# A three-stage token kernel on one core: the second stage in seven products of quarters, with three weights decoded early and staged in DRAM

## The chip, the cores and the metric

The kernel runs on one core of one Trainium2 chip. The metric is device time in microseconds (us) of one execution. The core has separate instruction streams for TensorE (PE, with its weight loads as PEld), VectorE (DVE), ScalarE (ACT), GpSimd (POOL) and SyncE (SP, which issues nearly all DMAs here). The fast memory on the core is SBUF, matmul results go to PSUM, and the chip's DRAM holds inputs, outputs and whatever is staged between.

## The reference

Attention gives 2304 tokens of 512 numbers each; two layers follow.

```python
x = attention(q, k, v)            # pooled (factor 4) attention plus a banded local one, 4 batches of 576 tokens
h = (x @ w_a) * (x @ w_b)         # 512 -> 1536
x2 = h @ w_out                    # 1536 -> 512, the second stage
g = x2 @ w_in                     # 512 -> 2048, the third
g = g * clip(g + 3, 0, 6) / 6
out = g @ w_out2                  # 2048 -> 512, the fourth
```

Weights arrive as 64-bit floats and are decoded on the chip into 32-bit ones. A product of float32 matrices is done in three passes: each operand is split in two parts of fewer bits (ACT copies the first part, DVE subtracts to get the second), and first x second, second x first and first x first are added up in PSUM.

## The kernel before

**The order of the work** comes from a planner. Every step (`PE`, `ACT`, `DVE` or `DMA`) is added with an estimated cost, a wanted time, the steps it follows and the buffers it takes and gives back. The planner then walks through time and issues, on each engine, the ready step that is wanted earliest; the engine executes them in just that order. Times in the plan only decide the order, and a wait on the chip is a semaphore.

**Stage 1** works on blocks of at most 384 tokens. Attention for two units of 116 tokens after the other makes the block's tile `x` (in two parts: `total` L603, `x_first` L611 on ACT, `x_second` L616 on DVE). Three such tiles exist. For a block, `job` runs through 12 column groups of w_a and w_b: two products of 12 matmuls each into `pab` (L663), a copy on ACT (L669), a multiplication on DVE (L672) and a store of `h` to DRAM (L675). Attention of the later blocks is woven between these products on PE: scores `sc` and `dsc`, transposes `pt` and `dpt`, and products with v, `po` L590 and `dpo`.

**Weights.** `decode` loads a tile of 128 x 1024 doubles (as two 32-bit words each) into one of three `raw` slots and makes floats of it: absolute value on ACT (L262), two exponent passes on DVE (L276, L277), a rounding pass on ACT (L270, some on DVE, L268), the upper word's pass L281 and the joining pass L287 on DVE. For w_a, w_b and w_out the two parts then go straight to SBUF (L291, L294). `pieces` decodes the second layer's first weight w_in, makes four sums of quarters on DVE (L330) and splits seven pieces (L339, L343). `staged` decodes the second layer's second weight, eight tiles, makes four differences of quarters (L1142) and writes seven pieces to DRAM in three DMAs (`w_d`), wanted from shortly before the time T1 in stage 1; stage 4 reads them back.

**Stage 2**, `second(n, f, want)`, goes through spans of 512 tokens (four, and one of 256) and, in each, through 12 tiles of `h`: a load (L704), the split on ACT (L708) and DVE (L712), and 4 x 3 matmuls into four PSUM banks (L720). After the twelfth tile ACT copies the result out (L752) and it goes to DRAM as `x2_d`.

**Stages 3 and 4** already work in seven products of quarters: two blocks of 384 tokens and two halves of the inner dimension form a 2 x 2 matrix of blocks, and seven products in place of eight, of sums and differences, give the result. `inner` and its `group` do it with 1008 matmuls of 384 columns (L848), `outer` with 1512 of 256 (L972, L987). The operands are split at L775 and L778 after a subtraction of 128x768 (L784); the results are put together at L857, L865, L873 and L876.

Of the kernel before, what the change touches and what calls it, by code (L numbers as in the profile page):

```python
# [9 lines left out]
F32 = mybir.dt.float32  # L10
# [144 lines left out]
def fused_kernel(ctx: ExitStack, tc: tile.TileContext, qk, vt, vd, wab, wo, w2i, w2o, mask, out):  # L155
# [33 lines left out]
    def fill():  # L189
        if not unread:  # L190
# [8 lines left out]
            "eT": 2, "xf": 2, "x": 3, "a": 3, "b": 4, "s2": 2, "wo": F1 // 2, "w2": 2, "hg0": 2,  # L199
            "hg1": 2, "xo": 3, "q": 8, "ws": 1, "x0": 4, "L": 24, "c": 14}  # L200
# [3 lines left out]
    plan.loose |= {"b", "turn", "pv", "m", "s2", "e", "de", "eT", "deT", "xf", "dqk", "a", "q", "xo", "c"}  # L204
# [37 lines left out]
    wab_t, wo_t, w2_t = {}, {}, {}  # L242
# [69 lines left out]
    takers = {}  # L312

    def pieces(src, want, where, raw=None, step=CUT):


        i, words = decode(src, want, None, None, slack=1.0, raw=raw, step=step)
        Q = W // CUT

        def quarters():  # L320
            lo, hi = words()
            return (hi.bitcast(F32).rearrange("p (a c) -> p a c", a=CUT),
                    lo.bitcast(F32).rearrange("p (a c) -> p a c", a=CUT))

        def sums():
            v, e = quarters()
            for k, (x, y, op) in enumerate(
                    ((v[:, 2], v[:, 3], ALU.add), (e[:, 0], v[:, 0], ALU.subtract),
                     (v[:, 0], v[:, 2], ALU.subtract), (v[:, 1], e[:, 1], ALU.subtract))):
                nc.vector.tensor_tensor(e[:, k], x, y, op=op)  # L330

        i = DVE(4 * dve(Q), want, sums, [i], slack=1.0)

        ends = []
        for at, of, q, n in ((0, 0, 0, 2), (2, 0, 3, 1), (3, 1, 0, 4)):
            for a, b, key, tag, before, place in where(at, at + n):
                def first(a=a, b=b, of=of, q=q + a - at, place=place):
                    x = quarters()[of][:, q:q + b - a]
                    nc.scalar.activation(place(0), x, AF.Copy)  # L339

                def second(a=a, b=b, of=of, q=q + a - at, place=place):
                    x = quarters()[of][:, q:q + b - a]
                    nc.vector.tensor_tensor(place(1), x, place(0), op=ALU.subtract)  # L343

                n_ = (b - a) * Q
                j = ACT(act(n_), want, first, [i, *before, takers.get(key)], take=[tag] if tag else [], slack=1.0)
                takers.setdefault(key, j)
                ends.append(DVE(dve(n_), want, second, [j]))
        return plan.add("-", 0, want, lambda: None, ends, give=[raw or "raw"])

# [334 lines left out]

    cuts = list(range(0, NT, NC)) + [NT]
    spans = list(zip(cuts, cuts[1:]))
    hs, accs, x2_d = {}, {}, {}

    def hg_slot(n, f, name):  # L690
        if n == 0 and f in EDGE:
            return slot(xp, [P, 2, NC], F32R, "x", name)
        return slot(pools["p3" if f % 4 > 1 else "p2"], [P, 2, NC], F32R, f"hg{f % 4 // 2}", name)

# [3 lines left out]
    def second(n, f, want):  # L698
        lo, hi = spans[n]
        nb = hi - lo  # L700

        def load():
            h = hs[n, f] = hg_slot(n, f, "h")[:, :, :nb]
            nc.sync.dma_start(h[:, 1].bitcast(F32), h_d[f][:, lo:hi])  # L704

        def h_first():
            h = hs[n, f]
            nc.scalar.activation(h[:, 0], h[:, 1].bitcast(F32), AF.Copy)  # L708

        def h_second():  # L710
            h = hs[n, f]
            nc.vector.tensor_tensor(h[:, 1], h[:, 1].bitcast(F32), h[:, 0], op=ALU.subtract)  # L712
# [10 lines left out]
        edge = n == 0 and f in EDGE  # L723
        hg = "x" if edge else f"hg{f % 4 // 2}"
        stored = [x for m in range(NBLK) if begin[m] < hi and begin[m] + sizes[m] > lo for x in S_["h", m, f]]
        i = DMA(nb // 2, want - 40, load, stored + ([] if edge else [S_["p3" if f % 4 > 1 else "p2"]]), take=[hg])
        i = ACT(act(nb), want - 14, h_first, [i])
        i = DVE(dve(nb), want - 14, h_second, [i])
        busy = 12 * (0.0134 + nb / 2400)
        end = n == len(spans) - 1  # L730
        take, give = ["q"] * KC if f == 0 else [], [hg]
        if end and f >= F1 - 3:

            i = S_["issued", f] = PE(0.01, want - 3, products, [i, S_["wo", f // 2], S_["ps"], S_.get(("issued", f - 1))],
                                     take=take, slack=-PE_L)
            i = PE(busy, want, lambda: None, [i], give=give)
        else:
            i = PE(busy, want, products, [i, S_["wo", f // 2], S_["ps"], S_["second", n, 0] if f else None], take=take, give=give)
        S_["second", n, f] = i
        if f < F1 - 1:  # L740
            return
        if end:
            S_["p4"] = plan.add("-", 0, 0, open_p4, [S_["issued", f]] +
                                [issued[x] for m in range(2 * PAIRS) for x in S_.get(("x2d", m), [])] +
                                [issued[x] for k in range(F2 // 2) for x in S_["w_d", k]])
        for e in range(KC):
            T = {}

            def out_of(e=e, T=T):
                T["t"] = (slot(pools["p4"], [P, NB], F32, "c", "x2f") if end else  # L750
                          slot(pools["p3"], [P, NC], F32, "xo", "x2f"))[:, :nb]
                nc.scalar.activation(T["t"], accs[n][e], AF.Copy)  # L752

            def store(e=e, T=T):
                for m in range(lo // NB, (hi - 1) // NB + 1):
                    if m not in x2_d:
                        x2_d[m] = dram.tile([KC, P, NB], F32, name=f"x2_d{m}")
                    a, b = max(lo, m * NB), min(hi, m * NB + NB)
                    nc.sync.dma_start(x2_d[m][e][:, a - m * NB:b - m * NB], T["t"][:, a - lo:b - lo])

            tag = "c" if end else "xo"
            j = ACT(act(nb), want, out_of, [i, S_["p4"] if end else None], take=[tag], give=["q"])
            j = DMA(nb // 2, want, store, [j], give=[tag])
            for m in range(lo // NB, (hi - 1) // NB + 1):
                S_.setdefault(("x2d", m), []).append(j)
# [20 lines left out]
    def inner(p, want, opened):  # L786
# [49 lines left out]
    def group(p, i, want, X, ready):  # L836
# [3 lines left out]
        def product(k, w, give=(), onto=None, after=()):  # L840
# [10 lines left out]
            return PE(6 * (0.0134 + NB / 2400), w, run, ready[k] + [S_["w2i", i], S_["ps"], *after],  # L851
# [266 lines left out]
    w_d = [dram.tile([P, 7, CUT, W // CUT], F32, name=f"w_d{h}") for h in range(F2 // 2 // CUT)]  # L1118

    def staged(k, want):  # L1120
        i, words = decode(w2o[k], want, None, None, slack=1.0, step=1)
        T = {}

# [205 lines left out]
```

## Time and profile before

| | before |
|---|---|
| runs shown (us) | 941.47, 940.19, 939.75; median 940.19 |
| the profiled execution: its time (us) | 938.81 |
| its span, first to last instruction (us) | 936.7 |
| PE busy | 925.9 us, 99% of the span |
| PEld busy | 867.6 us, 93% |
| DVE busy | 659.2 us, 70% |
| ACT busy | 511.2 us, 55% |
| DMA, mean over the span | 161 GB/s |

Start and end of the profiled execution lie 2.1 us outside its span. Busy time is time in which an engine had an instruction in it, so it is a share of the whole, over stages with different limits; matmuls are pipelined, so that one matmul's own duration (335 ns, say) is longer than the distance from one to the next. The stages follow each other in time: stage 1 to 425.9 us, stage 2 to 576.9 us, stage 3 to 752.2 us, then stage 4.

### The profile page before, as it was taken

To read this page: it belongs to the slowest core of one execution; us is meant where nothing else is said; L and a number is where in the kernel's file an instruction comes from. 1 tells how busy PE (TensorE), PEld (TensorE's weight loads), DVE (VectorE), ACT (ScalarE), POOL (GpSimd) and SP (SyncE) were. 2 spreads that over 40 slices of the span, in tenths; PEclk is the share of its full clock that TensorE was granted. 3 is DMA by queue.
4 is the path that set the end of the run, shared out by engine and by line. 5 is a ranking of instruction groups with operands and counts; after the bars stand their busy time and mean duration, and the time that the engine had idled before them with its cause. 6 is when DMAs were issued, how large, how long until landed. Compare 5 with 4: busy or idle time off the path is not lost.

```text
span 936.7 us, 18571 instructions
## 1 busy us (share of the span) xinstructions
PE 925.9 (99%) x7040; PEld 867.6 (93%) x7040; DVE 659.2 (70%) x1231; ACT 511.2 (55%) x1242; POOL 3.2 (0%) x40
## 2 busy tenths in 40 slices
PE   9999999999999999999999999999999999999998
PEld 6678899999999999997888889999999999999998
DVE  5999967767967677789222224777556799897983
ACT  3768744557557654455322324666566775454551
POOL 0000000000000000000000000000000000000000
PEclk9999999999999999999999999999999999999999
DMA  9734845555554454554434544525257782706401
GB/s 299 238 121 158 284 169 170 169 170 169 192 182 162 130 190 140 180 159 129 135 100 137 140 122 133 186 94 194 103 182 244 265 265 72 261 7 208 130 19 51
DMA packets 102440, 151.20 MB, mean 161 GB/s; under 512 B 8784, under 2 KB 70992, under 8 KB 102352
## 3 DMA queue, kind: packets, MB, share of 16 engines
q1 hardware_dynamic: 101632, 148.80, 49.2%
q8 instruction: 55, 0.90, 0.4%
q10 hardware_dynamic: 720, 1.23, 0.4%
q14 instruction: 33, 0.27, 0.1%
HBM read 100.19 MB, written 49.81 MB: 160 GB/s over the span
## 4 chain that ended last, share of the span: by engine, by line
PE 92%; DVE 5%; DMA 1%; ACT 1%; issue 0%; SPq 0%; POOL 0%; ACTq 0%; POOLq 0%; DVEq 0%
PE pab L663 31%; PE ph L848 19%; PE oacc L987 18%; PE acc L720 16%; PE po L590 2%; PE dsc L433 2%; PE dpo L483 1%; PE oacc L972 1%; PE sc L534 1%; PE dpt L465 1%; PE unread L192 1%; PE pt L575 1%; DMA raw<-w2o 1%; DVE dqk L423 1%; DVE raw L287 0%; DVE m L281 0%
## 5 line engine op out<-in xcount | busy, mean ns | idle before, releaser
L663 PE MATMUL pab<-x,wh 128*128 128x384 f32 (+2 forms) x1776 | 320.2, 337 | 0.1
L663 PEld LDWEIGHTS pab<-x,wh 128*128 128x128 f32 x1776 | 302.0, 188 | 3.4 <-issue 1.3
L848 PE MATMUL ph<-in,w 128*128 128x384 f32 x1008 | 175.3, 335 | 0.0
L848 PEld LDWEIGHTS ph<-in,w 128*128 128x128 f32 x1008 | 175.1, 188 | 0.0
L987 PE MATMUL oacc<-w2o,in 128*128 128x256 f32 x1440 | 172.6, 283 | 0.0
L987 PEld LDWEIGHTS oacc<-w2o,in 128*128 128x128 f32 x1440 | 172.6, 192 | 0.0
L720 PE MATMUL acc<-h,wo 128*128 128x512 f32 (+1 forms) x720 | 150.9, 371 | 1.4 <-DVE a L672 1.1
L720 PEld LDWEIGHTS acc<-h,wo 128*128 128x128 f32 x720 | 125.4, 188 | 27.0 <-DVE a L672 1.4
L712 DVE TENSOR_TENSOR h<-h 128x512 fp32r<-128x512 f32 (+1 forms) x60 | 38.1, 638 | 98.2 <-ACT h L708 98.2
L708 ACT ACTIVATE h<-h 128x512 fp32r<-128x512 f32 (+1 forms) x60 | 35.3, 589 | 94.1 <-DMA h<-h_d 57.5
L672 DVE TENSOR_TENSOR a<-a,pab 128x384 f32<-128x384 f32 (+2 forms) x74 | 40.0, 540 | 59.4 <-PE pab L663 31.7
L669 ACT ACTIVATE a<-pab 128x384 f32<-128x384 f32 (+2 forms) x74 | 35.6, 480 | 81.4 <-PE pab L663 70.9
L775 ACT ACTIVATE in<-gr 128x384 fp32r<-128x384 f32 x96 | 47.3, 520 | 41.7 <-PE oacc L987 27.3
L865 DVE TENSOR_TENSOR part<-ph,part 128x384 f32<-128x384 f32 x72 | 39.8, 555 | 32.5 <-PE ph L848 21.2
L873 ACT ACTIVATE r<-part,three 128x384 f32<-128x384 f32 x72 | 43.9, 615 | 27.4 <-DVE part L865 26.5
L778 DVE TENSOR_TENSOR in<-gr,in 128x384 fp32r<-128x384 f32 x96 | 49.6, 551 | 8.0 <-ACT in L775 7.5
L775 ACT ACTIVATE in<-e 128x384 fp32r<-128x384 f32 x72 | 37.1, 524 | 29.1 <-PE oacc L987 22.7
L857 ACT ACTIVATE part<-ph 128x384 f32<-128x384 f32 x72 | 35.2, 490 | 27.0 <-PE ph L848 25.2
L262 ACT ACTIVATE m<-raw 128x1024 f32<-128x1024 f32 x34 | 38.8, 1140 | 7.0 <-DMA raw<-w2o 2.6
L281 DVE SCALAR_TENSOR_TENSOR m<-raw,m 128x1024 uint32<-128x1024 uint32 x34 | 41.4, 1218 | 0.3
L287 DVE CUSTOM_DVE_ANT_0 raw<-raw,m 128x2048 uint16<-128x2048 uint16 x34 | 41.3, 1216 | 0.3
L876 DVE SCALAR_TENSOR_TENSOR r<-r,part 128x384 f32<-128x384 f32 x72 | 38.8, 549 | 0.9 <-ACT r L873 0.9
(97 smaller groups left out, 966.8 us busy)
## 6 DMA issues: line engine op xcount, KB each, us to landing
g_d<-r SPq DMA_DIRECT2D x96, 192.0 KB
gr<-g_d SPq DMA_DIRECT2D x48, 384.0 KB
h_d<-a SPq DMA_DIRECT2D x70, 192.0 KB
raw<-wab SPq DMA_DIRECT2D x12, 1024.0 KB
h<-h_d SPq DMA_DIRECT2D x48, 256.0 KB
raw<-w2o SPq DMA_DIRECT2D x32, 256.0 KB
w2o<-w_d SPq DMA_DIRECT2D x14, 512.0 KB
qk<-qk SPq DMA_DIRECT2D x12, 576.0 KB
```

The lines of the kernel that those rows point to most:

```text
L262: nc.scalar.activation(T["m"], words()[1].bitcast(F32), AF.Abs)
L281: nc.vector.scalar_tensor_tensor(out=mu, in0=words()[1], scalar=0xC0000000, in1=mu, op0=ALU.bitwise_and, op1=ALU.bitwise_or)
L287: nc.vector.tensor_tensor(hi, T["m"].bitcast(U32), lo, op=ALU.add)
L663: nc.tensor.matmul(T[k], wab_t[f][:, x, c], xs[n][:, g, y, ja:jb], start=(g == 0 and i == 0), stop=(g == KC - 1 and i == 2))
L672: nc.vector.tensor_tensor(T["a"], T["a"], T[1], op=ALU.mult)
L720: nc.tensor.matmul(accs[n][e], wo_t[f // 2][:, x, c], hs[n, f][:, y], start=(f == 0 and i == 0), stop=(f == F1 - 1 and i == 2))
L775: nc.scalar.activation(x[0][:, 0], src(), AF.Copy)
L778: nc.vector.tensor_tensor(x[0][:, 1], src(), x[0][:, 0], op=ALU.subtract)
L848: nc.tensor.matmul(acc[k], t[:, x, g * P:(g + 1) * P], X[k, g][0][:, y], start=(g == 0 and n == 0 and not onto), stop=(g == 1 and n == 2), ...
L865: nc.vector.tensor_tensor(s[name], acc[k], s[other], op=ALU.add)
L873: nc.scalar.activation(T["r"], src(), AF.Relu, bias=three)
L987: nc.tensor.matmul(acc[n][e], X[n, k][0][:, x, e * P:(e + 1) * P], t[:, y], start=(k == 0 and i == 0), stop=(k == K - 1 and i == 2))
```

## The change

**Stage 2** becomes `middle(p)`, three times, each for a pair of 384-token blocks. h for a pair (two blocks of tokens, t = 0 and 1) and w_out are both cut into quarters (the inner dimension in two halves of six tiles), and seven products are formed in the order 1, 5, 6, 3, 7, 2, 4. Each product is three steps (kk) of 12 matmuls of 384 columns (two tiles of h, two of the four output tiles, three passes), 36 in all; so 63 steps and 756 matmuls stand where 720 stood, 576 of them of 512 columns and 144 of 256. `load` brings four DMAs of 192 KB per kk and block of tokens, the first block into `h0`, the second into a `raw` slot of `decode`. For each product `sub` subtracts on DVE in place where a difference is wanted, and `parts` splits into one of six `X` slots, 128x768 each time. `keep` copies a PSUM result to SBUF on ACT, `add` adds the next product's to it on DVE, and products marked `onto` go on in the same PSUM bank.

**Weights.** w_out and w_in are now `staged` as well, before the second layer's second weight: 22 tiles in all, wanted from T1 - LEAD - SOON on, one every PACE. A tile is decoded in its `raw` slot, four sums or differences are written on DVE (L1170), three quarters copied on ACT (L1173), and the seven pieces leave as one DMA of 896 KB; `raw` is given back when that has landed. `loaded` brings them back as tiles `wt` of 512 KB, 11 for w_out and 14 for w_in, and splits them on ACT (L1230) and DVE (L1234). `pieces` and the direct way of w_out go.

The core of the diff:

```diff
-            "eT": 2, "xf": 2, "x": 3, "a": 3, "b": 4, "s2": 2, "wo": F1 // 2, "w2": 2, "hg0": 2,
-            "hg1": 2, "xo": 3, "q": 8, "ws": 1, "x0": 4, "L": 24, "c": 14}
+            "eT": 2, "xf": 2, "x": 3, "a": 3, "b": 4, "s2": 2, "h0": 3, "X": 6, "y": 8, "w2": 2, "q": 8, "x0": 4, "L": 24,
+            "c": 14}
...
-        def products():
-            if f == 0:
-                accs[n] = [bank("acc")[:, :nb] for _ in range(KC)]
-            for e in range(KC):
-                c = slice(f % 2 * DM + e * P, f % 2 * DM + (e + 1) * P)
-                for i, (x, y) in enumerate(PASSES):
-                    nc.tensor.matmul(accs[n][e], wo_t[f // 2][:, x, c], hs[n, f][:, y],
-                                     start=(f == 0 and i == 0), stop=(f == F1 - 1 and i == 2))
...
+            e1 = parts(1, kk, b11, [l0])
+            t1 = sub(5, b11, b12, b11, [e1, l1])
+            e5 = parts(5, kk, b11, [t1])
+            t2 = sub(6, b11, b22, b11, [e5])
+            e6 = parts(6, kk, b11, [t2])
+            e3 = parts(3, kk, b22, [l1])
+            t3 = sub(7, b12, b22, b12, [e3, t1])
+            e7 = parts(7, kk, b12, [t3])
+            plan.add("-", 0, want, lambda: None, [e7, t2], give=["raw"])
+            e2 = parts(2, kk, b21, [l0])
+            t4 = sub(4, b11, b21, b11, [e2, e6])
+            e4 = parts(4, kk, b11, [t4])
...
+                    for j in range(2):
+                        t = wo_t[(c0 + j) // CUT][:, (c0 + j) % CUT]
+                        for e in range(2):
+                            for i, (x, y) in enumerate(PASSES):
+                                nc.tensor.matmul(acc[n][e], t[:, x, e * P:(e + 1) * P], X[n, kk][:, j, y],
+                                                 start=(kk == 0 and j == 0 and i == 0 and not onto),
+                                                 stop=(kk == KK - 1 and j == 1 and i == 2), skip_group_check=n != 2)
...
-    for k in range(F2 // 2):
-        S_["w_d", k] = staged(k, T1 - 16 + 2.4 * k)
+        j = ACT(act(3 * Q), want, copy, [i])
+        k = DVE(4 * dve(Q), want, sums, [i], slack=0.3)
+        plan.add("-", 0, want, lambda: None, [j, k], give=["dm"])
+        return [DMA(896, want, lambda: nc.sync.dma_start(dest, r7()), [j, k], give=["raw"])]
...
+        S_[name, k] = staged(src[k], T1 - LEAD - SOON + PACE * i, dest(), name == "w_d")
...
+        S_["wo", j] = loaded((T2 - 34 + 2.5 * j, T2 - 30 + 2.5 * j), "wh", parts_, made, lambda t, j=j: wo_t.setdefault(j, t))
```

How this moves instructions shows best in stage 1, where block 3 of the tokens (the fourth block) begins. In before, the stream of DVE there has the last split of that block's `x` (L616, twice) among work for the block being multiplied (L672) and for attention:

```order
L672 TENSOR_TENSOR a<-a,pab 128x384
L423 TENSOR_REDUCE dqk<-qk 128x288
L1142 TENSOR_TENSOR ws<-raw,ws 128x256
L281 SCALAR_TENSOR_TENSOR m<-raw,m 128x1024
L603 TENSOR_TENSOR xf<-po,od 128x464
L565 TENSOR_SCALAR z<-z 128x8
L566 RECIPROCAL z<-z 128x8
L438 TENSOR_REDUCE dmx<-dsc 72x4
L441 TENSOR_SCALAR dmx<-dmx 72x4
L616 TENSOR_TENSOR x<-xf,x 128x4x36
L616 TENSOR_TENSOR x<-xf,x 128x4x80
L375 TENSOR_TENSOR e<-e,z 128x512
```

In the changed kernel the same split (now L578) has four decode passes (L277, L278, L282, L289) and a row maximum (L511, L512) between it and the multiplication ahead (now L634), which is the last one of block 2:

```order
L634 TENSOR_TENSOR a<-a,pab 128x384
L277 TENSOR_SCALAR m<-m 128x1024
L278 TENSOR_SCALAR m<-m 128x1024
L511 TENSOR_REDUCE mx<-e 128x8
L512 TENSOR_SCALAR mx<-mx 128x8
L282 SCALAR_TENSOR_TENSOR m<-raw,m 128x1024
L565 TENSOR_TENSOR xf<-po,od 128x464
L289 ISA m<-raw,m 128x2048
L578 TENSOR_TENSOR x<-xf,x 128x4x36
L578 TENSOR_TENSOR x<-xf,x 128x4x80
L400 TENSOR_REDUCE dmx<-dsc 72x4
L403 TENSOR_SCALAR dmx<-dmx 72x4
```

The split has moved back, behind the end of block 2's products. On PE, in before, block 3's last attention product `po_3110` is followed by five more products of block 2 (`x_1550`) and some attention work; the first product of block 3, `pab_3325<-x_2820`, comes four rows after this piece:

```order
L590 MATMUL po_3110<-eT_3099,vz1_104 64x58 x16
L433 MATMUL dsc_3134<-dqk_3106 72x144 x4
L663 MATMUL pab_3145<-x_1550,wh_1807 128x384 x12
L663 MATMUL pab_3175<-x_1550,wh_2014 128x384 x12
L575 MATMUL pt_3193<-ident_81,e_3041 128x128 x4
L663 MATMUL pab_3202<-x_1550,wh_2014 128x384 x12
L590 MATMUL po_3220<-eT_3217,vz0_103 64x58 x16
L465 MATMUL dpt_3241<-ident_81,de_3167 72x72 x4
L433 MATMUL dsc_3247<-dqk_3190 72x144 x4
L663 MATMUL pab_3255<-x_1550,wh_2098 128x384 x12
L465 MATMUL dpt_3283<-ident_81,de_3167 72x72 x4
L663 MATMUL pab_3288<-x_1550,wh_2098 128x384 x12
```

In the changed kernel that attention product (`po_3236`) comes after the last product of block 2 (`x_1560`), and the first of block 3 (`x_2880`) right behind it:

```order
L625 MATMUL pab_3145<-x_1560,wh_2160 128x384 x12
L625 MATMUL pab_3170<-x_1560,wh_2355 128x384 x12
L625 MATMUL pab_3196<-x_1560,wh_2355 128x384 x12
L537 MATMUL pt_3221<-ident_81,e_3068 128x128 x4
L395 MATMUL dsc_3229<-dqk_3218 72x144 x4
L552 MATMUL po_3236<-eT_3226,vz1_104 64x58 x16
L625 MATMUL pab_3281<-x_2880,wh_434 128x384 x12
L625 MATMUL pab_3311<-x_2880,wh_434 128x384 x12
L625 MATMUL pab_3334<-x_2880,wh_640 128x384 x12
```

Between block 3's last attention product and its first use there is nothing left on PE. The third place is DVE early in stage 2 of the changed kernel, with the differences (L700), the second parts (L683) and second parts of weights (L1234):

```order
L700 TENSOR_TENSOR hr<-hr 128x768 x2
L683 TENSOR_TENSOR hx<-hr,hx 128x2x384 x3
L700 TENSOR_TENSOR hr<-hr 128x768
L1234 TENSOR_TENSOR wt<-wt 128x4x256 x2
L683 TENSOR_TENSOR hx<-hr,hx 128x2x384 x3
L700 TENSOR_TENSOR hr<-hr 128x768
L683 TENSOR_TENSOR hx<-hr,hx 128x2x384
L700 TENSOR_TENSOR hr<-hr 128x768
L683 TENSOR_TENSOR hx<-hr,hx 128x2x384
L700 TENSOR_TENSOR hr<-hr 128x768
L683 TENSOR_TENSOR hx<-hr,hx 128x2x384
L1234 TENSOR_TENSOR wt<-wt 128x4x256
```

Where before DVE had one second part (L712) for twelve matmuls, it now has one of 128x768 and, for more than every second step, a difference of the same size as well, in turns.

## Rows read from the trace of the kernel before

**Rows 1.** Cores: span, mean granted TensorE clock.
```profile
core 0: 936.7 us, clock 1.000
```
**Rows 2.** Chain of work that ended last: start us, us, what.
```profile
425.88 136.12 PE acc L720 x600
...
577.07 175.18 PE ph L848 x1008
```
**Rows 3.** Windows: us, then PE, PEld, DVE, ACT, POOL busy; PEclk, DMA share, GB/s.
```profile
80.00:245.00 165.00, 164.15 (x1459) 153.94 (x1458) 127.99 (x222) 100.55 (x293) 1.27 (x16) 1.00 0.58 191
425.90:576.90 151.00, 150.70 (x720) 125.40 (x721) 52.22 (x85) 49.41 (x84) 0.00 (x0) 1.00 0.44 129
576.90:752.20 175.30, 175.30 (x1011) 175.30 (x1010) 123.28 (x231) 115.85 (x224) 0.00 (x0) 1.00 0.52 176
```
**Rows 4.** Lines by form, PE and PEld: busy us, mean ns, idle before.
```profile
L848 PE MATMUL ph<-in,w 128*128 128x384 f32 x1008 | 175.3, 335 | 0.0
L848 PEld LDWEIGHTS ph<-in,w 128*128 128x128 f32 x1008 | 175.1, 188 | 0.0
...
L720 PEld LDWEIGHTS acc<-h,wo 128*128 128x128 f32 x720 | 125.4, 188 | 27.0 <-DVE a L672 1.4 <-ACT h L708 0.4 <-DVE h L712 0.3
```
**Rows 5.** Timeline of DVE around 245 us: start us, us, operation.
```profile
245.05 0.70 DVE L616 TENSOR_TENSOR x<-xf,x 128x144 fp32r<-128x144 f32 x2
```
**Rows 6.** Timeline of PE from 236 to 260 us: start us, us, operation.
```profile
247.38 0.60 PE L575 MATMUL pt<-ident,e 128*128 128x128 f32 x4
...
249.98 1.14 PE L590 MATMUL po<-eT,vz 64*64 64x58 f32 x32
...
257.45 0.71 PE L433 MATMUL dsc<-dqk 64*72 64x144 f32 x8
258.09 2.18 PE L663 MATMUL pab<-x,wh 128*128 128x384 f32 x11
```
**Rows 7.** Lines by form, DVE operations of stage 1.
```profile
L281 DVE SCALAR_TENSOR_TENSOR m<-raw,m 128x1024 uint32<-128x1024 uint32 x34 | 41.4, 1218 | 0.3
L287 DVE CUSTOM_DVE_ANT_0 raw<-raw,m 128x2048 uint16<-128x2048 uint16 x34 | 41.3, 1216 | 0.3
...
L672 DVE TENSOR_TENSOR a<-a,pab 128x384 f32<-128x384 f32 x70 | 38.6, 551 | 58.5 <-PE pab L663 31.0 <-ACT m L262 12.2 <-ACT wo L291 4.9
...
L277 DVE TENSOR_SCALAR m<-m 128x1024 uint32<-128x1024 uint32 x34 | 23.6, 694 | 1.2
L276 DVE TENSOR_SCALAR m<-m 128x1024 f32<-128x1024 f32 x34 | 23.2, 682 | 1.1 <-ACT m L262 1.1
...
L330 DVE TENSOR_TENSOR raw<-raw 128x256 f32<-128x256 f32 x32 | 12.1, 421 | 0.3
...
L549 DVE TENSOR_REDUCE mx<-e 128x8 f32<-128x512 f32 x10 | 6.7, 673 | 0.0
...
L603 DVE TENSOR_TENSOR xf<-po,od 128x464 f32<-128x464 f32 x9 | 5.6, 625 | 2.0 <-PE po L590 1.5 <-PE sc L534 0.5
...
L550 DVE TENSOR_SCALAR mx<-mx 128x8 f32<-128x8 f32 x20 | 3.4, 171 | 0.7
```
**Rows 8.** Waits: who waited for whom, us in total, times, longest.
```profile
DVE h L712 <- ACT h L708: 98.2, 52, 3.1
...
PE acc L720 <- DVE a L672: 1.1, 1, 1.1
```
**Rows 9.** Lines by form: operations of the sizes that the new stage uses.
```profile
L865 DVE TENSOR_TENSOR part<-ph,part 128x384 f32<-128x384 f32 x72 | 39.8, 555 | 32.5 <-PE ph L848 21.2 <-ACT in L775 5.2 <-ACT part L857 5.2
...
L1250 DVE TENSOR_TENSOR w2o<-w2o 128x1024 fp32r<-128x1024 f32 x14 | 17.0, 1216 | 1.0 <-ACT w2o L1246 1.0
...
L784 DVE TENSOR_TENSOR x2r<-x2r 128x768 f32<-128x768 f32 x12 | 11.4, 953 | 0.1
...
L339 ACT ACTIVATE w<-raw 128x768 fp32r<-128x768 f32 x4 | 3.6, 910 | 1.1 <-PE pab L663 1.1
```
**Rows 10.** The page's slices of 23.4 us: what the DMA engines moved.
```profile
GB/s 299 238 121 158 284 169 170 169 170 169 192 182 162 130 190 140 180 159 129 135 100 137 140 122 133 186 94 194 103 182 244 265 265 72 261 7 208 130 19 51
```

More of the change, by code (lines that the diff above doesn't have):

```diff
@@ L36 @@
 MEAN = 332
-NC = 512
-EDGE = (2, 3)
 TAIL = 4
+LEAD = 24
+SOON = 14
+PACE = 2.4
 FILL = 0.4
@@ L239, in DMA @@
         return j
[L242 removed]
+    wab_t, w2_t = {}, {}
     pools = {}
@@ L305, in decode @@
         i = DVE(dve(W), want, upper, [i])
-        i = DVE(dve(W), want, both, [i, r], give=["dm"], slack=slack)
+        i = DVE(dve(W), want, both, [i, r], give=[] if put is None else ["dm"], slack=slack)
         if put is None:
-            return i, words
+            return i, T
         i = ACT(act(W), want, first, [i, *after], take=[tag], slack=slack)
         return DVE(dve(W), want, second, [i], give=[raw or "raw"])
[L312 to L349, printed above, removed]
     vz = [ap.tile([P, 2, HP, D], F32, name=f"vz{i}") for i in range(2)]
@@ L683, in job @@
         S_.setdefault(("h", n, f), []).append(DMA(nb // 2, want - 50, store, [i], give=["a"]))
[L686 to L693, printed above, removed]
+    x2_d = {}
     def bank(name):
         return slot(pools["ps"], [P, BANK], F32, "q", name)
[L698 to L712, printed above, removed]
-        def products():
-            if f == 0:
-                accs[n] = [bank("acc")[:, :nb] for _ in range(KC)]
-            for e in range(KC):
-                c = slice(f % 2 * DM + e * P, f % 2 * DM + (e + 1) * P)
-                for i, (x, y) in enumerate(PASSES):
-                    nc.tensor.matmul(accs[n][e], wo_t[f // 2][:, x, c], hs[n, f][:, y],
-                                     start=(f == 0 and i == 0), stop=(f == F1 - 1 and i == 2))
[L723 to L765, printed above, removed]
@@ L1235, in fused_kernel, with loaded, load, first @@
-    T3 = T2 + len(steps)
+    S_["p3"] = plan.add("-", 0, 0, open_p3, [x for n, f, _ in jobs[-2:] for x in S_["h", n, f]])
+    def loaded(want, tag, pieces_, after, keep):
+        T = {}
+        def load():
+            T["t"] = slot(wpool if tag == "wh" else pools["pw"], [P, CUT, 2, Q], F32R, tag, "wt")
+            keep(T["t"])
+            for a, n, src in pieces_:
+                nc.sync.dma_start(T["t"][:, a:a + n, 1].bitcast(F32), src)
+            T["n"] = sum(n for _, n, _ in pieces_)
+        def first():
+            t = T["t"][:, :T["n"]]
+            nc.scalar.activation(t[:, :, 0], t[:, :, 1].bitcast(F32), AF.Copy)
+        def second():
+            t = T["t"][:, :T["n"]]
+            nc.vector.tensor_tensor(t[:, :, 1], t[:, :, 1].bitcast(F32), t[:, :, 0], op=ALU.subtract)
+        n = sum(n for _, n, _ in pieces_)
+        i = DMA(128 * n, want[0], load, after + ([] if tag == "wh" else [S_["p3"]]), take=[tag])
+        i = ACT(act(n * Q), want[1], first, [i])
+        return DVE(dve(n * Q), want[1], second, [i])
@@ new lines, in fused_kernel @@
+    made = [x for k in range(F1 // 2) for x in S_["wo_d", k]]
+    for j in range(-(-W1 // CUT)):
+        parts_, c = [], j * CUT
+        while c < min(W1, j * CUT + CUT):
+            rank, k = divmod(c, F1 // 2)
+            n = min(F1 // 2 - k, j * CUT + CUT - c)
+            parts_.append((c - j * CUT, n, wo_d[:, AS_A[ORDER[rank]], k:k + n]))
+            c += n
+        S_["wo", j] = loaded((T2 - 34 + 2.5 * j, T2 - 30 + 2.5 * j), "wh", parts_, made, lambda t, j=j: wo_t.setdefault(j, t))
```

230 lines of the change are left out of this document (152 added, 78 removed).

## The prediction

> **What bounds the kernel now.** First the cores: the granted TensorE clock is 1.000 over the whole span of 936.7 us [rows 1], which is the upper of its two levels, 2.4 GHz, so nothing can be gained or explained there as yet. Then the chain of waits: stages 2 and 3 are in it as long unbroken runs of matmuls [rows 2]. Then the windows of the stages [rows 3]: in stage 2 PE is busy for 150.7 of 151.0 us while DVE works 52.2 and ACT 49.4; in stage 3 PE is busy all the time, DVE 123.3 and ACT 115.9 of 175.3 us. So PE ends last in both, and time goes only where PE gets less to do, or where a feeder falls behind. Between 80 and 245 us, in stage 1, DVE works 128.0 of 165.0 us; that is the narrowest place for what the change adds.
>
> I work from the profiled execution, 938.81 us, which is 1.4 us below the median of the runs shown (940.19); that is added at the end. One measurement of this kernel can tell about 0.2%, 1.9 us, from no change.
>
> **Gain: stage 2 on PE.** 720 matmuls in 151.0 us go; 756 of 384 columns come. Stage 3 is a whole stage of that very form and gives the distance from one to the next: 175.3 us / 1008 = 0.1739 us [rows 4]. 756 x 0.1739 = 131.5 us, so 151.0 - 131.5 = **19.5 us** are saved, if everything arrives in time.
>
> Weight loads give another price. They are busy for 125.4 us in stage 2 and for 175.1 of 175.3 us in stage 3, 188 ns each [rows 4]. If each of the 756 took its 188 ns by itself, they would set the pace: 142.1 us, and only 8.9 saved. Against that, 1008 loads of 188 ns are 189.5 us and went through in 175.3, overlapping; so I take 19.5 and keep 8.9 as a rival. The Trainium skill ("Perfetto Trace Analysis", section "Identifying the Most-Contended Engine") holds matmul busy time to be a poor measure of the room left on this engine and wants the busy time of the weight loads looked at. By that rule stage 2 still had room, and the new stage has none.
>
> **Loss 1: the join of block 3 in stage 1.** The staging of w_out and w_in is pulled forward. Ahead of the split of block 3's `x`, DVE gets 22 more quarter sums, 4 more of each of the passes L276, L277 and L281, 5 more L287 and 3 more multiplications, and loses two small operations of 0.9 us: 22 x 0.421 + 4 x (0.682 + 0.694 + 1.218) + 5 x 1.216 + 3 x 0.551 - 0.9 = 26.5 us [rows 7] (the quarter sums priced by L330, of the same 128x256). DVE has 165.0 - 128.0 = 37.0 us idle before 245 us [rows 3], and block 3 is now ready early: its last columns end at 245.75 [rows 5], its first product starts at 258.09 [rows 6], 12.3 us ahead. Bounds: 0 if the idle time swallows enough, 26.5 - 12.3 = 14.2 us if it swallows nothing. The order decides between them: the split now stands behind the last multiplication of block 2, which cannot start before block 2's last product has ended. From there DVE has in a row a multiplication 0.551, two exponent passes 0.694 and 0.682, a maximum 0.673 + 0.171, L281 1.218, the sum `xf` 0.625, L287 1.216 and the two splits 0.70: 6.53 us [rows 5, 7]. Successive DVE operations overlap by some 0.08 us, so 5.9; the hand-over from PE and back costs the 1.1 us that PE waited at the end of stage 1 for one such multiplication less its 0.55 [rows 7, 8], so 6.4. In that time PE has a transpose 0.60, scores 0.71 and the attention product 1.14 [rows 6], less overlap 2.3. **4.2 us** of PE idle is my value.
>
> Block 3's products before T1 and the rest of stage 1 stay as they are, and so do the 1.1 us at the change of PSUM pools [rows 8].
>
> **Loss 2: the start of stage 2.** X for the first products needs h of two blocks, and the loads of the second go into `raw` slots that a store of 896 KB has to free. DVE has for the whole stage 63 second parts and 36 differences of 128x768, 18 additions of 128x384 and 11 second parts of weights: 99 x 0.953 + 18 x 0.555 + 11 x 1.216 = 117.7 us against 131.5 on PE; ACT has 63 x 0.910 plus 24 results and 11 first parts, below that [rows 9]. It fits, with six slots of X in hand, but with 14 us to spare only, so that a late start is not made up quickly. No row shows this start. Bounds: 0, and one chain through a late load: an ACT copy 0.91, a difference and a second part 0.95 each, 2.8 us. I take **1.0**, since the order has the first parts of the pair ahead of stage 1's end.
>
> **Loss 3: into stage 3.** Its first operands need the last blocks of `x2`, and DVE has to do the last additions, then splits, then w_in's second parts. Before there were 0.3 us of PE idle here. Bounds 0 and 2.1 (an addition, a difference and a split, 0.555 + 0.953 + 0.555); I take **0.8**.
>
> **At nothing**, with the cover: in stage 3 the 14 second parts of w_in, 14 x 1.216 = 17.0 us [rows 9], raise DVE from 123.3 to at most 140.3 of 175.3, so 35 us of cover remain. The DMAs: 22 stores of 896 KB instead of 8 are 12.8 MB more; over the 245 us from the beginning to block 3 that would be 52 GB/s beside the 191 that ran from 80 to 245 us [rows 3], where slices have shown 299 [rows 10]. Reading back 11 x 512 KB over 131 us adds 44 GB/s to 129, and 14 x 512 KB over 175 us 42 GB/s to 176. Were that cover gone, SP's queue would hold the slots of `raw`, which is the fourth rival. Stage 4 is not touched.
>
> **Sum:** -19.5 + 4.2 + 1.0 + 0.8 = -13.5 us. 938.81 - 13.5 = 925.3 for a profiled execution, **926.7** as the median.
>
> **Rivals.**
> 1. *No stall at block 3.* If ACT, the DMAs and PE run a little later than DVE does, the passes ahead of the split are done while PE is still in block 2. For it: 37 us of idle DVE. Against it: the split sits behind block 2's last multiplication in the order whatever the speed. 926.7 - 4.2 = 922.5.
> 2. *The clock falls.* PE had no idle stretch as long as 4.2 us in a run whose clock was 1.00 throughout [rows 1], so the trace doesn't show what one does. If it brought the lower level, 1.2 GHz, for as long as two products of 12, those would take 4.2 us more (24 x 0.1739): 930.9. The Trainium skill ("TensorE: Matmul & The Clock Gate", Part 1) says that idleness brings the half rate and activity releases it; no run before this one can show which stretch suffices here.
> 3. *Weight loads set the pace* of stage 2: 8.9 saved in place of 19.5, 926.7 + 10.6 = 937.3. Speaking for and against: above.
> 4. *Stage 1 falls further behind.* `raw` slots wait for stores, decoded weights come late, and the 26.5 us go into the front as a whole: 14.2 in place of 4.2, 936.7; half of that way is 931.7.
> 5. *Slower: copy and subtraction take turns in stage 2.* DVE waited 98.2 us in 52 waits for ACT's copies [rows 8], harmlessly, as it had time. Each of the 63 splits now needs a copy that follows, for most of them, a difference on DVE itself, and the order has L700 and L683 one after the other. If every copy's 0.91 were waited for on DVE, stage 2 would last 117.7 + 63 x 0.91 = 175.0 us, 43.5 more than forecast: 970.2. It decides from the point where DVE's 13.8 us of spare time are used up, 15 such waits; from 30 on the kernel is slower than before. Against it: two or three second parts stand in a row in the order, so that copies of another kk run ahead, into six slots.
> 6. *Hardly anything happens* (the new stage is starved in small pieces and gives the gain back): within 0.2%, 940.
>
> **How the numbers follow.** The forecast gets 0.57, rival 1 0.12, rival 2 0.09, rival 3 0.04, rival 4 0.10, rival 5 0.05, rival 6 0.03. The forecast's own bounds (join 3 to 6, start 0 to 2.8, stage 3 0 to 2.1) give 924 to 930. The range goes down to 921.5 for rival 1 with a smooth start (922.5 less 1.0), and up to 933.5, which takes in rival 2 and the milder half of rival 4; outside are rivals 3, 5, 6 and the worse half of 4, 0.17 together. Faster by over 0.2%: the forecast and rivals 1 to 4, 0.92; within: rival 6, 0.03; slower: rival 5, 0.05.
>
> **What would show it.** In the windows stage 2 should last 131 to 134 us with PEld busy nearly all of it, as in stage 3. The timeline of PE should show a gap near the end of block 2, some 255 us in, with DVE's x as its releaser, 3 to 6 us long; no such gap speaks for rival 1. The clock of the stretch behind it settles rival 2. Waits of L683 for ACT's copies that end in PE gaps would be rival 5. I am wrong if stage 2's matmuls are further apart than 0.176 us without gaps, or if PE waits in stage 1 for weights or loads instead of `x`.

## The result and the profile after

The changed kernel takes 924.75 us (median of 4 runs, 923.96 to 925.01); before, 940.83 in the same session. The ratio is 0.9826, with a 95% interval of 0.9808 to 0.9843: 16.1 us saved, where 13.5 were forecast, and 924.75 lies in the range. The profiled execution is 924.78 us, its span 923.0 against 936.7 before [rows 1].

The cores' view now has a clock that is no longer whole:

```profile
core 0: 923.0 us, clock 0.996
```

The chain of waits, start us, us, what, shows where the 13.7 us of the span are from. The lines answer to [rows 2]:

```profile
432.42 131.05 PE acc L729 x756
563.47 175.22 PE ph L876 x1008
```

Stage 2 lasts 131.05 us in one unbroken piece, where 425.88 to 577.07 were 151.19; that is 20.1 us less. Stage 3 follows at once and has kept its length. But stage 2 begins at 432.42 instead of 425.88: stage 1 gave 6.5 us back. In the windows (us, busy PE, PEld, DVE, ACT, POOL, then PEclk, DMA share, GB/s) the two new full stages and the place of the loss read:

```profile
432.30:563.40 131.10, 131.10 (x758) 131.10 (x757) 107.16 (x127) 70.20 (x96) 0.00 (x0) 1.00 0.54 174
563.40:738.60 175.20, 175.20 (x1010) 175.20 (x1009) 127.23 (x235) 118.07 (x226) 0.00 (x0) 1.00 0.54 182
245.00:270.00 25.00, 21.22 (x158) 19.76 (x148) 22.03 (x43) 12.98 (x44) 0.64 (x8) 0.86 0.77 271
```

Stage 2 is now of stage 3's kind: PE and weight loads busy all the time, DVE twice as busy as before (107.2 against 52.2 us, [rows 3]) and still not the bound. Between 245 and 270 us PE stands for 3.8 us, and its clock is 0.86 on average. The timeline of PE there, with the idle time before a piece and what ended it:

```profile
245.24 6.63 PE L625 MATMUL pab<-x,wh 128*128 128x384 f32 x36
251.71 0.60 PE L537 MATMUL pt<-ident,e 128*128 128x128 f32 x4
252.91 0.71 PE L395 MATMUL dsc<-dqk 64*72 64x144 f32 x8 [0.59 <-DVE dqk L385]
253.55 1.14 PE L552 MATMUL po<-eT,vz 64*64 64x58 f32 x32
257.57 0.69 PE L625 MATMUL pab<-x,wh 128*128 128x384 f32 x1 [2.88 <-ACT x L573]
258.56 6.69 PE L625 MATMUL pab<-x,wh 128*128 128x384 f32 x22 [0.31 <-DVE x L578]
```

and the one of DVE in the same microseconds:

```profile
251.50 1.35 DVE L385 TENSOR_REDUCE dqk<-qk 128x288 f32<-128x1152 f32 x1
252.77 0.54 DVE L634 TENSOR_TENSOR a<-a,pab 128x384 f32<-128x384 f32 x1
253.23 0.69 DVE L277 TENSOR_SCALAR m<-m 128x1024 f32<-128x1024 f32 x1
253.95 0.69 DVE L278 TENSOR_SCALAR m<-m 128x1024 uint32<-128x1024 uint32 x1
254.56 0.68 DVE L511 TENSOR_REDUCE mx<-e 128x8 f32<-128x512 f32 x1
255.28 0.17 DVE L512 TENSOR_SCALAR mx<-mx 128x8 f32<-128x8 f32 x1
255.38 1.23 DVE L282 SCALAR_TENSOR_TENSOR m<-raw,m 128x1024 uint32<-128x1024 uint32 x1
256.53 0.63 DVE L565 TENSOR_TENSOR xf<-po,od 128x464 f32<-128x464 f32 x1
257.08 1.21 DVE L289 CUSTOM_DVE_ANT_0 m<-raw,m 128x2048 uint16<-128x2048 uint16 x1
258.21 0.70 DVE L578 TENSOR_TENSOR x<-xf,x 128x144 fp32r<-128x144 f32 x2
```

This is the queue that the order showed, without a hole: the last multiplication of block 2, the decode passes, the sum `xf`, and block 3's split last. PE waited 0.59 + 2.88 + 0.31 = 3.8 us. The 0.59 are for another operation, L385, which also holds the multiplication back: block 2's last product ends at 251.87, and the multiplication starts at 252.77. The 2.88 end with ACT's first part of `x` (L573), for which DVE's `xf` (L565, done at 257.16) has to be there. And when PE went on, it went at the lower level, 1.2 GHz; three of the windows of 1 us:

```profile
257.00:258.00 1.00, 0.43 (x1) 0.28 (x1) 1.00 (x2) 0.81 (x3) 0.00 (x0) 0.73 0.89 313
260.00:261.00 1.00, 1.00 (x5) 1.00 (x5) 0.97 (x4) 1.00 (x7) 0.00 (x0) 0.50 0.48 184
264.00:265.00 1.00, 1.00 (x7) 1.00 (x6) 0.00 (x0) 0.00 (x0) 0.00 (x0) 0.85 0.32 129
```

All six between 258 and 264 us stand at 0.50, with PE at work in nearly all of that time.

For the comparisons below one more place is needed, where block 1 begins; from there to stage 2 no start-up differences count:

```profile
104.33 7.86 PE L625 MATMUL pab<-x,wh 128*128 128x384 f32 x43 [0.41 <-DVE x L578]
```

That is 432.42 - 104.33 = 328.1 us.

### The profile page after: what moved, and what is told of

Same layout as the page of the kernel before. It is cut to its first block, busy times and chain, and to the rows that moved or that the text cites. A ratio compares the mean times of both kernels' runs of the same rounds, so it can differ in the third digit from the quotient of the medians.

```text
span 923.0 us, 18730 instructions
## 1 busy us (share of the span) xinstructions
PE 909.5 (99%) x7076; PEld 876.7 (95%) x7076; DVE 733.5 (79%) x1299; ACT 537.1 (58%) x1234; POOL 3.2 (0%) x40
## 4 chain that ended last, share of the span: by engine, by line
PE 92%; DVE 5%; DMA 1%; issue 0%; ACT 0%; POOL 0%; SPq 0%; POOLq 0%; ACTq 0%; DVEq 0%
PE pab L625 32%; PE ph L876 19%; PE oacc L1015 19%; PE acc L729 14%; PE po L552 2%; DMA qk<-qk 1%; PE dsc L395 1%; PE dpo L445 1%; PE oacc L1000 1%; PE sc L496 1%; PE dpt L427 1%; PE unread L193 1%; DVE m L282 1%; DVE dqk L385 1%; PE pt L537 1%; DVE mx L511 0%
## 5 line engine op out<-in xcount | busy, mean ns | idle before, releaser
L625 PE MATMUL pab<-x,wh 128*128 128x384 f32 (+2 forms) x1776 | 323.9, 339 | 3.7 <-ACT x L573 2.9
L625 PEld LDWEIGHTS pab<-x,wh 128*128 128x128 f32 x1776 | 305.2, 190 | 7.3 <-ACT x L573 3.0
L876 PE MATMUL ph<-in,wt 128*128 128x384 f32 x1008 | 175.4, 335 | 0.0
L876 PEld LDWEIGHTS ph<-in,wt 128*128 128x128 f32 x1008 | 175.2, 188 | 0.0
L729 PE MATMUL acc<-hx,wt 128*128 128x384 f32 x756 | 131.2, 334 | 0.0
L729 PEld LDWEIGHTS acc<-hx,wt 128*128 128x128 f32 x756 | 131.1, 188 | 0.0
L634 DVE TENSOR_TENSOR a<-a,pab 128x384 f32<-128x384 f32 (+2 forms) x74 | 40.0, 541 | 54.6 <-PE pab L625 20.0
L680 ACT ACTIVATE hx<-hr 128x768 fp32r<-128x768 f32 x63 | 52.1, 844 | 40.9 <-PE acc L729 22.3
L683 DVE TENSOR_TENSOR hx<-hr,hx 128x768 fp32r<-128x768 f32 x63 | 58.7, 954 | 18.4 <-ACT hx L680 18.1
L282 DVE SCALAR_TENSOR_TENSOR m<-raw,m 128x1024 uint32<-128x1024 uint32 x34 | 41.5, 1220 | 0.5
L806 DVE TENSOR_TENSOR in<-e,in 128x384 fp32r<-128x384 f32 x72 | 37.8, 551 | 0.8 <-ACT in L803 0.5
```

The lines of the kernel that those rows point to most:

```text
L282: nc.vector.scalar_tensor_tensor(out=mu, in0=words()[1], scalar=0xC0000000, in1=mu, op0=ALU.bitwise_and, op1=ALU.bitwise_or)
L625: nc.tensor.matmul(T[k], wab_t[f][:, x, c], xs[n][:, g, y, ja:jb], start=(g == 0 and i == 0), stop=(g == KC - 1 and i == 2))
L634: nc.vector.tensor_tensor(T["a"], T["a"], T[1], op=ALU.mult)
L680: nc.scalar.activation(X[n, kk][:, :, 0], src(), AF.Copy)
L683: nc.vector.tensor_tensor(X[n, kk][:, :, 1], src(), X[n, kk][:, :, 0], op=ALU.subtract)
L729: nc.tensor.matmul(acc[n][e], t[:, x, e * P:(e + 1) * P], X[n, kk][:, j, y], start=(kk == 0 and j == 0 and i == 0 and not onto), stop=(kk ...
```

## The experiments

**Theory A**: the wait at block 3 comes from where its split stands in DVE's order, and the low clock is a consequence of the wait. **Rival B**: DVE has too much to do in stage 1, wherever the split stands. **Rival C**: the clock falls there by itself. Ratios are to the kernel before, with 95% intervals; a kernel without an interval had one run.

**Attention of block 3 earlier.** The staging stays as it is.

```diff
-        t = when[m, 0] - 4 + 0.1 * i if m < 3 else when[m - 3, F1 - 1] - 6 + 1.2 * i
+        t = when[m, 0] - 4 + 0.1 * i if m < 3 else when[m - 3, F1 - 1] - (10 if m == 3 else 6) + 1.2 * i
```

> Attention of block 3 alone is wanted 4 units earlier in the plan, so that its x stands ahead of block 2's last multiplications in DVE's order; the staged decoding stays as early and as much as in the change. Theory A (the position of the split in DVE's order makes the wait, and the low clock is a consequence of the wait): no gap at the join and clock 1.00 throughout, so the change's 3.8 us of gaps and 3.4 us of half clock both go: 924.8 - 7.2 = 917.6 us. Rival B (DVE has too much to do ahead of T1, so a wait of about the same length turns up at another place before 450 us): 923 to 925 us, DVE the releaser. Rival C (the clock falls by itself there, from DMA traffic for instance): the gap goes and the low clock stays: 921 us.

Measured: 918.66 us (917.87 to 919.22), 0.9769 (0.9755 to 0.9782), an interval below that of the change. The same window; the beginning of block 1 in the timeline; the beginning of stage 2 in the chain:

```profile
245.00:270.00 25.00, 25.00 (x184) 23.17 (x181) 20.79 (x40) 16.30 (x50) 0.00 (x0) 1.00 0.71 240
```
```profile
105.44 8.41 PE L625 MATMUL pab<-x,wh 128*128 128x384 f32 x47 [0.45 <-DVE x L578]
```
```profile
425.51 131.05 PE acc L729 x756
```

PE has no idle time between 245 and 270 us, the clock is 1.00, and from block 1 to stage 2 it takes 320.1 us, 8.0 fewer than the change: somewhat more than the 7.2 expected. Of the whole time less comes back, 6.1 us by the medians (924.75 to 918.66), since this execution reached block 1 1.1 us later than the change's and is the fastest of its four. The wait has not moved to another place: with the same staging, DVE has `x` ready in time in this order. B falls, and so does C in its simple form. The other three executions have a mean clock of 0.998 over the span; where it was lower in them is not shown.

**The gap filled with spare matmuls.** This separates the wait from the clock.

```diff
+                if (n, f, k) == (3, 0, 0):
+                    for _ in range(12):
+                        nc.tensor.matmul(bank_, ident16, ident16.unsqueeze(1).to_broadcast([P, BANK // P, P]), start=True, stop=True)
```

> The change with 12 spare matmuls (bf16, 512 columns, nobody reads them) ahead of block 3's first product, where PE waits; everything else in the same order. They take about 12 x 0.22 = 2.6 us of the 2.9 us gap. Theory A (clock follows the gap): x comes at the same time, PE's first product of block 3 starts at the same time within 0.3 us, but the clock stays at 1.00, and the 3.4 us come back: 921.4 us. Rival C (the clock falls for another reason): granted clock 0.5 for some 7 us as in the change, 924.8 us.

Measured: 922.2 us (922.07 to 922.5), 0.9808 (0.9794 to 0.9822). The timeline of PE:

```profile
254.51 2.76 PE L624 MATMUL pab<-ident 128*128 128x512 bf16 x12
257.45 0.44 PE L629 MATMUL pab<-x,wh 128*128 128x384 f32 x1 [0.18 <-ACT x L573]
258.45 3.74 PE L629 MATMUL pab<-x,wh 128*128 128x384 f32 x20 [0.56 <-DVE x L578]
```

and the window from 258 us on:

```profile
258.00:266.00 8.00, 7.55 (x48) 7.15 (x49) 7.85 (x19) 4.71 (x20) 0.00 (x0) 1.00 0.73 275
```

Block 3 begins 0.12 us from where it began in the change, so x was hardly earlier; but the clock is 1.00. So it is in all five executions (1.000 over the span), where the change's four have 0.996 to 0.998. Block 1 and stage 2 begin at:

```profile
104.58 8.42 PE L629 MATMUL pab<-x,wh 128*128 128x384 f32 x47 [0.45 <-DVE x L578]
```
```profile
429.70 131.05 PE acc L733 x756
```

325.1 us lie between them, against 328.1 in the change and 320.1 in the experiment before. So in the profiled executions the low clock alone cost **3.0 us**, and it follows PE's idle time; the wait itself cost **5.0 us**. The intervals of the whole times overlap here (the change's is 0.9808 to 0.9843), so the 3.0 rests on the two traces. Of the 5.0, 3.8 show as idle time. Part of the rest may be the matmuls at the edges of the wait, which have no neighbour to overlap with (the single one takes 0.44 us here, where 0.17 is the distance in a row); that is not shown.

**Less work for DVE, the order kept.** The first ten staged tiles get no quarter sums, so their pieces are not the reference's.

```diff
-            for k, (to, f, x, g, y) in enumerate(ops):
+            for k, (to, f, x, g, y) in enumerate(ops if spare else ()):
```

> The change without the four quarter sums of the first ten staged tiles (all six of w_out, the first four of w_in; their pieces hold other words, so the output is not the reference's): 40 DVE operations of 0.42 us fewer ahead of block 3, some 14 us net, all others in the same order. Theory A (the split waits behind block 2's last multiplication, whatever DVE's load): gap at the join 2.5 to 3.8 us, clock falls as before: 923 to 925 us. Rival B (DVE's load makes the gap): DVE runs 10 us or more ahead, x is there in time, gap under 0.5 us, clock 1.00: 917.6 us.

Measured: 923.34 us (923.17 to 924.85), 0.9822 (0.9809 to 0.9836): as the change. PE and then DVE:

```profile
257.00 0.44 PE L625 MATMUL pab<-x,wh 128*128 128x384 f32 x1 [2.64 <-ACT x L573]
258.00 7.87 PE L625 MATMUL pab<-x,wh 128*128 128x384 f32 x35 [0.56 <-DVE x L578]
```
```profile
250.70 1.35 DVE L385 TENSOR_REDUCE dqk<-qk 128x288 f32<-128x1152 f32 x1 [0.39 <-DMA qk<-qk]
252.19 0.56 DVE L634 TENSOR_TENSOR a<-a,pab 128x384 f32<-128x384 f32 x1
257.64 0.70 DVE L578 TENSOR_TENSOR x<-xf,x 128x144 fp32r<-128x144 f32 x2
```

40 operations fewer, and DVE even idle ahead of L385, yet the multiplication starts only when block 2's product is there (252.10), and the split comes 5.45 us behind it, where it was 5.44 in the change. The gap is 2.64 + 0.56 = 3.2 us, and the clock falls again:

```profile
258.00:266.00 8.00, 8.00 (x38) 7.96 (x39) 6.79 (x16) 3.44 (x15) 0.00 (x0) 0.79 0.64 245
```

So 3.2 of the 3.8 us stay as long as the position does. The other 0.6 went with the load: the wait for L385 is gone. The low clock is shorter here, added up from windows of 1 us 3.4 us in place of 6.8 (the change has 0.61 in the window shown).

**Staging later**: `LEAD = 18` in place of 24.

> LEAD 18 in place of 24: all 22 staged tiles are wanted 6 units later. Theory A: fewer decode passes stand ahead of block 3's x, no gap at the join (-7.2 us); but w_out's tiles come back later, and PE waits at the start of stage 2, up to 5 us with the low clock behind it if the gap is over 3 us: 918 to 925 us, with the gap moved to 430 to 445 us, loads or weight splits as releaser. Rival B (load, not order): the gap at the join shrinks by no more than the share of tiles that moved, 1 us or so, and stage 2 starts without a wait: 923 to 925 us.

Measured: 920.82 us (919.87 to 921.01), 0.979 (0.9776 to 0.9804). No gap at block 3; 11.7 us into stage 2 instead, after 60 matmuls:

```profile
437.25 0.44 PE L729 MATMUL acc<-hx,wt 128*128 128x384 f32 x1 [1.31 <-ACT hx L680]
438.24 121.14 PE L729 MATMUL acc<-hx,wt 128*128 128x384 f32 x695 [0.55 <-DVE hx L683]
```

A wait comes as theory A has it, smaller than its upper end and with no lower clock behind it (1.000 over the span). But neither loads nor weight splits end it; it ends with the split of `h`, whose copies (L680) stand on ACT behind a first part of w_in and behind two results (L757) for which ACT waits until 435.45, shortly before PE stops:

```profile
432.57 1.06 ACT L1230 ACTIVATE wt<-wt 128x1024 fp32r<-128x1024 f32 x1 [4.04 <-DMA wt<-wi_d]
435.45 1.01 ACT L757 ACTIVATE x2f<-acc 128x384 f32<-128x384 f32 x2 [1.82 <-PE acc L729]
436.36 2.30 ACT L680 ACTIVATE hx<-hr 128x768 fp32r<-128x768 f32 x3
```

The 3 us of the expectation is a bound that no run shows. So the lead buys stage 2's smooth start; that w_out's tiles come back late is not what this trace shows, and how the later staging led to this order stays open.

**Three slots of X**: `"X": 3` in place of 6.

> The change with three slots of X in place of six (the planner's order follows that). Theory A (six slots let ACT's copies and DVE's second parts run ahead, which is why rival 5 did not come): with three slots a copy can start only when the product two steps before has ended; PE waits for L683 in many of the 63 steps, stage 2 grows from 131 us by 5 to 15, the whole to 930 to 940 us. Rival (two steps ahead, 4.2 us, are enough for a copy 0.84 and a second part 0.95): 924 to 926 us, and stage 2 stays at 131 to 132 us.

Measured: 929.04 us (one run). Of its 4.3 us above the change, 2.3 are from stage 1: stage 2 begins at 434.73, and PE was 2.5 us late where block 1 begins (106.8 us), long before X is used. About 1 us of that was there before 47 us; the rest comes with a low clock from 51 us on. The window here and in the change:

```profile
51.00:55.00 4.00, 4.00 (x22) 2.81 (x23) 3.93 (x8) 3.25 (x11) 0.00 (x0) 0.57 0.00 0
51.00:55.00 4.00, 4.00 (x55) 3.26 (x53) 3.93 (x7) 4.00 (x17) 0.00 (x0) 1.00 0.09 32
```

Ahead of this both have the same wait of 1.57 us, so a wait of that length was followed by a fall in one kernel and not in the other. Stage 2 itself:

```profile
434.70:567.70 133.00, 132.15 (x758) 131.01 (x757) 110.58 (x130) 72.72 (x98) 0.00 (x0) 1.00 0.54 172
```

133.0 us, 1.9 more than with six slots. Two steps ahead are nearly enough; by this run six slots are not what kept rival 5 away. My expectation was too high, though the sign was right.

**DVE's room in stage 2**: second parts written twice, in two of the seven products and then in all.

```diff
-                nc.vector.tensor_tensor(X[n, kk][:, :, 1], src(), X[n, kk][:, :, 0], op=ALU.subtract)
+                for _ in range(2 if n in (5, 2) else 1):
+                    nc.vector.tensor_tensor(X[n, kk][:, :, 1], src(), X[n, kk][:, :, 0], op=ALU.subtract)
```

> The change with the second parts of products 5 and 2 written twice (the same values): 18 more DVE operations of 0.95 us in stage 2, 17 us by their durations, 15.5 by their distance of 0.87. By the prediction's own sum DVE has 13.8 us to spare in stage 2, and PE would wait 2 to 4 us: 927 to 929 us. By the window of the changed kernel DVE works 107.2 of 131.1 us there, 24 us are free, and 15.5 hide: 924 to 925.5 us with stage 2 at 131 us.

> The change with all 63 second parts written twice: 63 x 0.87 = 55 us more on DVE in stage 2. DVE then has 107 + 55 = 162 us to do against 131 on PE, so it becomes the bound: stage 2 about 160 us, the whole 924.8 + 29 = 954 us (by durations of 0.95, 960). If copies by ACT had been the limit (turns of copy and second part, rival 5), each doubled second part would add its 0.87 in full: 924.8 + 55 = 980 us.

With 18 more: 929.7 us (929.23 to 930.48), 0.9884 (0.9868 to 0.9901). Its window of stage 2 and the waits in PE's timeline:

```profile
433.00:569.00 136.00, 132.33 (x759) 131.12 (x758) 122.05 (x144) 68.63 (x96) 0.00 (x0) 1.00 0.52 168
```
```profile
470.25 87.88 PE L730 MATMUL acc<-hx,wt 128*128 128x384 f32 x504 [1.23 <-DVE x2f L767]
560.57 8.59 PE L730 MATMUL acc<-hx,wt 128*128 128x384 f32 x48 [2.44 <-DVE x2f L767]
```

Stage 2 is 4.7 us longer than in the change. DVE's 122 us would fit into 131, and still PE waits 3.7 us for additions alone: the additions (L766 in the change, L767 here) stand behind the second parts in DVE's order, and PE cannot go on with the next product in that bank before them. Both of my values were too low; the 24 us that the window shows as free are not free at those places.

With 63 more: 967.85 us (one run). The group of stage 2's matmuls (busy, mean ns, idle before) and the window:

```profile
L730 PE MATMUL acc<-hx,wt 128*128 128x384 f32 x756 | 144.3, 353 | 30.3 <-DVE x2f L767 17.4 <-ACT x2f L758 8.1 <-DVE hx L684 4.7
```
```profile
433.00:606.00 173.00, 142.65 (x749) 138.94 (x749) 160.52 (x185) 69.00 (x96) 0.00 (x0) 0.92 0.41 129
```

The waits are 30.3 us, what a DVE with 162 us of work leaves (29 expected); turns of copy and second part would have given 55. The other 13 us, which the expectation of 954 us lacked, are matmuls that take 144.3 instead of 131.2, at a mean clock of 0.92: waits are paid for twice.

**Banks of the first products exchanged.** Products 1 and 5 of the first pair change places in PSUM.

```diff
+                        if (p, n) == (0, 1):
+                            acc[5] = [bank("acc")[:, :NB] for _ in range(2)]
```

> The change with the PSUM banks of the first pair's products 1 and 5 exchanged, so that stage 2 begins in banks 2 and 3 of the new pool instead of 0 and 1. Before, PE waited 1.1 us there for the last multiplication of stage 1; in the change it does not. Theory (it does not wait because its first two banks are not those that the last products of stage 1 stand in; before, the first four banks were taken at once): a gap of 0.6 to 1.2 us at the start of stage 2, DVE's L634 the releaser, 925.5 to 926 us in all. Rival (the gap is gone because the last multiplication itself is earlier): no gap, 924.8 us.

Measured: 924.51 us (one run), and no gap at the start of stage 2, so the theory fell as it was put. Why the 1.1 us of [rows 8] went stays open: in the change the last multiplication of stage 1 runs from 432.52 on, beside stage 2, so PE no longer waits for it, but none of the first four banks was shown to be the cause.

Stage 1 of this kernel has the change's order and its wait (0.39 + 2.88 + 0.55 us), and yet half its low clock:

```profile
258.00:266.00 8.00, 7.14 (x30) 6.88 (x31) 6.71 (x16) 4.66 (x20) 0.00 (x0) 0.79 0.66 260
```

From block 1 (105.44) to stage 2 (432.12) it takes 326.7 us, 1.4 fewer than the change. So what the clock costs behind one and the same wait was 1.6 us here and 3.0 in the change, against the 325.1 of the filled gap; why it differs stays open.

**A better version.** Block 3's attention wanted 5 units earlier, `LEAD = 23`, `PACE = 2.2`.

> Block 3's attention wanted 5 units earlier, LEAD 23, PACE 2.2: staging begins one unit later and its tiles follow each other more closely. Theory A: no gap at the join as with 4 units earlier alone (about 918.2 us), stage 2 starts without a wait since the last staged tile is as early as before; the small gap of 0.4 us near 105 us can go too: 917.5 to 918.5 us. Rival (LEAD may not be cut at all): a gap of 1 us or more at the start of stage 2, 919 to 920 us.

Measured: 917.16 us (916.72 to 918.3), 0.9755 (0.9742 to 0.9769). The two windows:

```profile
245.00:270.00 25.00, 25.00 (x197) 23.09 (x197) 19.89 (x39) 16.07 (x48) 0.00 (x0) 1.00 0.71 249
424.70:555.70 131.00, 131.00 (x757) 131.00 (x757) 109.01 (x129) 69.74 (x96) 0.00 (x0) 1.00 0.56 178
```

PE has no idle time in either, nor a wait near 105 us. Clear of the change, not clear of the first experiment (0.9755 to 0.9782).

## Why the prediction was right, and where it was not

| term, us | forecast | measured | by |
|---|---|---|---|
| stage 2 on PE | -19.5 | -20.1 | chain, 151.19 to 131.05 |
| join of block 3, wait | +4.2 | +5.0, of it 3.8 idle | filled gap against earlier attention |
| lower clock behind it | a rival, +4.2 | +3.0 (1.6 with exchanged banks) | change against filled gap |
| start of stage 2 | +1.0 | 0 | no gap in the timeline |
| into stage 3 | +0.8 | 0 | no gap in the timeline |
| change of PSUM pools | 0 | -1.1 | no gap, 1.1 before |
| all else, to the span's 13.7 less | 0 | -0.5 | remainder |

The measured column is of the profiled executions.

**The gain** came as worked out: 131.05 / 756 = 0.1733 us from one matmul to the next, against 0.1739 from stage 3. Rival 3 fell: the loads are busy for 131.1 us and still 188 ns each, so they overlap as in [rows 4]. The Trainium skill ("Perfetto Trace Analysis", "Identifying the Most-Contended Engine") is borne out in its view: by weight loads stage 2 had room before (125.4 of 151.0) and has none now, while PE's busy share was 99% or more in both.

**The join** was right in mechanism and near in size. It was found in the order, and three experiments point to the same cause: without the position (first) or with later staging (fourth) the gap is gone, and with less load (third) 3.2 of 3.8 us stay. What the sum left out is L385, ahead of the multiplication: with its wait gone, the 0.6 us went. In return it counted as idle the time of the first matmul of block 3, which went ahead on ACT's first part (0.69 us).

**The step that failed** is the place of rival 2. I put the low clock beside the forecast as another case, with 0.09, where it was part of it: in all six kernels that kept the wait at block 3 unfilled (2.64 to 2.88 us in its longest piece), the clock fell there. The sum lacked 3.0 us, and the wait cost 0.8 more than put, though its idle time, 3.8, was below the 4.2. The Trainium skill ("TensorE: Matmul & The Clock Gate", Part 1) says that idleness brings the half rate; the runs agree for these waits, and show no fall after 1.31 and 0.55 us in the kernel with the later staging. They give no length that decides: after 1.57 us the clock fell in one kernel and not in the change.

**Losses 2 and 3** were put at 1.8 us together and are nothing. I priced two chains for which the planner had left time. That error, the pool wait (1.1) and a gain 0.6 larger hide the missing clock: the sum was right within 0.5 us, -13.5 against the -14.0 of the profiled executions (938.81 to 924.78), by errors that cancel; that closeness is luck. The last step, adding 1.4 us for the median, was wrong too: the profiled execution of the change lies at its own median, that of before lay below its. With `LEAD = 18` a wait of 1.9 us did come early in stage 2, so loss 2 was not priced without cause. The 0.3 us of idle from which loss 3 starts lay in stage 2, 10 us ahead of stage 3, where a split of h ended 0.23 us of it (at 566.50).

**Rivals 1 and 4** fell by the timeline: the gap was there, near the forecast's size. Rival 5 fell: PE has no idle time in stage 2, and with twice the second parts its waits fit DVE's sum and not turns with ACT. But its point of decision, 13.8 us of spare time, came out too generous: 15.5 us of added work made stage 2 4.7 us longer where 1.7 would be left over, since additions that PE waits for stand behind it.

## What to carry to other kernels

Work that is pulled forward into an engine's idle time can cost little by its amount (here 0.6 of 3.8 us of waiting) and much by its position: look for the one operation that the bound engine needs next, and count what stands ahead of it in the fixed order. A wait of the matmul engine should be priced with the clock behind it: here 5.0 us, and 1.6 to 3.0 more for the clock. Spare time summed over a stage is no cover for a place in it.

## What the runs showed that was not expected

- One wait of 2.9 us (and 0.3 behind it) was followed by six whole windows of 1 us at 0.50 of the clock, and the same wait with exchanged banks by half of that; after 1.3 and 0.6 us with one matmul between, the clock stayed at 1.00. Twelve unread matmuls in the wait kept it at 1.00.
- In the kernel that waits often (30.3 us in stage 2), matmuls themselves took 13.1 us more at a mean clock of 0.92.
- DVE's operations of 128x768 measure 0.95 us each and follow each other every 0.87 in a row. So 93 of the 99 and the rest that fell into stage 2's window were 107.2 us of busy time, where their durations add up to 115.3. The forecast's 117.7 added up durations, and six of the 99 lay outside the window.
